# Cutting the last weight loads of a gated attention-and-MLP decode step, and turning its heads one block sooner

## The chip, the cores and the metric

The kernel runs on 1 core of one Trainium2 chip. The metric is the device time of one execution in microseconds (us), as the median of several; a profile of one execution stands beside it. A ratio of two kernels is the mean time of one kernel's fast runs over that of the other's in the same rounds, so it is not quite the ratio of the medians quoted. Engine names: PE is the matmul engine, PEld its weight loads, DVE, ACT and POOL the elementwise engines, SP the engine that issues the loads. "DMA engine" means one of the 16 that move the bytes.

## The reference, cut to what matters

```python
# x: 4 x 1 x 1024; k_cache, v_cache: 4 x 32 x 8192 x 128; wq: 1024 x 4096; wo: 4096 x 1024; bfloat16
g = sigmoid((x * gate_w).sum(-1))
q = x @ wq
o = softmax(q @ k_cache^T / sqrt(128)) @ v_cache       # per batch and head, one query
a = o.reshape(4, 1, 4096) @ wo                         # <- the change is in this product's loads
b = x + gated_mlp(x)                                   # 1024 -> 3584 -> 1024, scaled by a sigmoid
return g * a + (1 - g) * b                             # 4 x 1 x 1024
```

Two caches of 268 MB each are read once, so the step is a stream of loads with a little arithmetic on each byte. The product with wo is the last thing that happens.

## The kernel before: the parts that matter

wo is cut into 8 blocks (`NWB`) of 512 rows. A block is 4 rows (`FR`) of 1024 columns in each of 128 partitions, that is 8 KB a partition and 1 MB in all. Each of its rows takes two matmuls of 512 columns (`NH = 2`) that accumulate into `acc`.

```python
def wo_block(g, r0=0, r1=FR):
    ...                                                # a place w in the ring of buffers
    nc.sync.dma_start(out=w[:, r0:r1]..., in_=wov[:, g, r0:r1]...)
    def use():
        for r in range(r0, r1):
            for n in range(NH):
                mm_acc(n, LT[:, r, g, :], w[:, r, n * NB:(n + 1) * NB])
    return use
```

The left operand `LT` comes from the attention output: the V product lies in PSUM, ACT and DVE bring it to `OS`, `flush()` turns the V sums on PE (8 short matmuls, "led<-selg,OS"), `flush_late()` scales them into `OT`, and `o_rows()` turns the heads into `LT` (16 short matmuls, "led<-OT,identb"). The heads of the last V pairs are needed by blocks 6 and 7 alone (`GE = 6`). The end of the kernel:

```python
    last = [wo_block(g) for g in range(2, NWB - 2)]                       # blocks 2..5 whole
    cuts = [(NWB - 2, 0, 2), (NWB - 2, 2, 4), (NWB - 1, 0, 2), (NWB - 1, 2, 3), (NWB - 1, 3, 4)]
    last += [wo_block(*cut) for cut in cuts]                              # 6 in halves; 7: half, row, row
    flush_sums()
    for g in range(2, GE):
        last.pop(0)()
        if g == 3:
            flush(); flush_late()
        if g == 4:
            o_rows(GE, NWB)
    for use in last:
        use()
    res = [turned(Bn, NB) for _ in range(NH)]
    nc.vector.tensor_copy(out=res[0], in_=acc(0));  nc.sync.dma_start(out=out2[:, 0:NB], in_=res[0])
    nc.scalar.copy(out=res[1], in_=acc(1));         nc.scalar.dma_start(out=out2[:, NB:D], in_=res[1])
```

## Time and profile before

| | |
|---|---|
| time | 1343.43 us, median of 3 runs, 1343.15 to 1343.82 |
| span of the profiled execution | 1341.4 us |
| load queue, share of 16 DMA engines' span | 99.5% |
| busiest compute engine | PE, 79% |
| last wo row complete on every DMA engine | 1337.68 us |
| second half's copy out of PSUM (ACT) begins | 1338.37 us |

How to read it: the load queue is busy for 99.5% of the span and no compute engine for more than 79%, so I take the time as bytes over rate plus what happens after the last byte (576.13 MB, at a mean of 429 GB/s).

### The profile page before, as it was taken

The numbers are of one execution on the slowest core, as the hardware profiler recorded it, in microseconds if no ns is written. First come the engines' busy times: TensorE is split into PE (matmuls) and PEld (weight loads), VectorE is DVE, ScalarE is ACT, GpSimd is POOL, SyncE is SP. The second block draws the span as 40 slices with busy tenths as digits, with TensorE's granted clock in tenths as the row PEclk, the third lists the DMA queues.
The fourth block names the chain that finished last, engine by engine and source line by source line (L and its number), as shares of the span: only waits on it lengthen the run. The fifth ranks groups of instructions, "written<-read, shape, count | busy, mean of one in ns | idle before, by whom it ended". The sixth has DMA issues, their size and how long they took to land.

```text
span 1341.4 us, 6922 instructions
## 1 busy us (share of the span) xinstructions
PE 1057.9 (79%) x4608; PEld 138.4 (10%) x1396; DVE 638.3 (48%) x386; ACT 66.2 (5%) x99; POOL 71.8 (5%) x209
## 2 busy tenths in 40 slices
PE   2565877887778789787879778789697879888888
PEld 0000000001001010101001010101011011111111
DVE  2555988556544347454436256646145556100000
ACT  0000000200000000100000000100000000111000
POOL 2000000100000001000000000100000000100000
PEclk9777989898989898888899888889898889889989
DMA  9999999999999999999999999999999999999998
GB/s 415 434 434 436 435 436 424 445 425 428 436 436 427 440 434 423 442 428 434 438 427 434 432 436 434 434 430 423 436 431 439 436 421 441 430 427 430 427 427 335
DMA packets 14890, 576.13 MB, mean 429 GB/s; under 512 B 1662, under 2 KB 1670, under 8 KB 2316
## 3 DMA queue, kind: packets, MB, share of 16 engines
q1 hardware_dynamic: 14852, 575.69, 99.5%
q8 instruction: 23, 0.38, 0.1%
q14 instruction: 7, 0.06, 0.0%
q10 hardware_dynamic: 8, 0.00, 0.0%
HBM read 575.68 MB, written 0.01 MB: 429 GB/s over the span
## 4 chain that ended last, share of the span: by engine, by line
DMA 67%; DVE 21%; PE 11%; issue 0%; ACT 0%; SPq 0%; DVEq 0%
DMA ring<-in_A_k_cache_dram 51%; DVE TB L453 19%; DMA ring<-in_A_v_cache_dram 12%; PE o_ps L537 7%; PE S_ps L458 3%; DMA ring<-in_B_w_gate_dram 3%; DVE OS L558 2%; DMA ring<-in_A_wo_dram 1%; PE o_ps L320 0%; DVE PT L494 0%; DVE mx L480 0%; PE acc L286 0%; PE led L574 0%; PE o_ps L574 0%; DVE OS L566 0%
## 5 line engine op out<-in xcount | busy, mean ns | idle before, releaser
L453 DVE STREAM_TRANSPOSE TB<-ring 128x2048 uint32<-128x2048 uint32 x256 | 568.3, 2278 | 472.6 <-DMA ring<-in_A_k_cache_dram 464.5
L458 PE MATMUL S_ps<-TB,Z 128*128 128x512 bf16 x2048 | 532.6, 415 | 191.4 <-DVE TB L453 183.6
L537 PE MATMUL o_ps<-ring,PB 128*64 128x512 bf16 x2048 | 462.8, 388 | 50.3 <-DMA ring<-in_A_v_cache_dram 49.0
L458 PEld LDWEIGHTS <-Z 128*128 128x128 bf16 x512 | 53.1, 104 | 656.0 <-issue 656.0
L537 PEld LDWEIGHTS <-PB 128*64 128x64 bf16 x512 | 57.1, 112 | 449.1 <-issue 446.4
L513 POOL COPY PB<-PT 32x256 bf16<-32x256 bf16 x64 | 39.1, 611 | 712.5 <-PE o_ps L537 519.4
L566 DVE SCALAR_TENSOR_TENSOR OS<-o_ps,mE,OS 128x512 f32<-128x512 f32 x5 | 3.8, 750 | 138.9 <-ACT OS L564 138.9
L511 ACT COPY PB<-PT 32x256 bf16<-32x256 bf16 x64 | 39.6, 619 | 256.8 <-PE o_ps L537 251.0
L435 POOL COPY Z<-qa 32x4 bf16<-32x4 bf16 x128 | 25.8, 201 | 459.8 <-PE S_ps L458 432.2
L554 ACT ACTIVATE OS<-o_ps,mE 128x512 f32<-128x512 f32 x11 | 7.6, 687 | 450.9 <-PE o_ps L537 450.9
L558 DVE SCALAR_TENSOR_TENSOR OS<-o_ps,mE,OS 128x512 f32<-128x512 f32 x33 | 24.3, 737 | 1.5
L489 ACT ACTIVATE TB<-S_ps,mx 128x2048 bf16<-128x2048 f32 x4 | 7.9, 1967 | 331.6 <-DVE mx L486 331.6
L286 PE MATMUL acc<-ring,hT 128*4 128x512 bf16 x56 | 14.7, 432 | 5.4 <-ACT TB L489 5.4
L244 PE MATMUL S_ps<-identb,x 6*128 6x6 bf16 x8 | 0.6, 196 | 22.5 <-DMA x<-in_gate_w_dram 22.5
L286 PE MATMUL acc<-ring,LT 128*4 128x512 bf16 x64 | 14.8, 378 | 1.9 <-DMA ring<-in_A_wo_dram 1.2
L574 PEld LDWEIGHTS o_ps<-selg,OS 128*128 128x128 f32 x88 | 11.5, 191 | 9.3 <-issue 8.8
L494 DVE STREAM_TRANSPOSE PT<-TB 128x2048 bf16<-128x2048 bf16 x4 | 9.2, 2311 | 6.4 <-ACT TB L489 6.4
L480 DVE TENSOR_REDUCE mx<-S_ps 128x1 f32<-128x2048 f32 x4 | 9.1, 2282 | 6.2 <-PE S_ps L458 6.2
L320 PE MATMUL o_ps<-ring,xw 128*4 128x512 bf16 x112 | 9.0, 444 | 3.7 <-DMA ring<-in_B_w_gate_dram 3.7
L574 PE MATMUL o_ps<-selg,OS 128*128 128x8 f32 x88 | 10.5, 245 | 0.0
L586 DVE SCALAR_TENSOR_TENSOR OT<-led,sgb,rinv 128x8 bf16<-128x8 f32 x5 | 1.2, 236 | 19.1 <-PE led L574 19.0
L564 ACT ACTIVATE OS<-o_ps,mE 128x512 f32<-128x512 f32 x5 | 3.4, 687 | 128.9 <-PE o_ps L537 128.9
(73 smaller groups left out, 83.0 us busy)
## 6 DMA issues: line engine op xcount, KB each, us to landing
ring<-in_A_v_cache_dram SPq DMA_DIRECT2D x18, 4096.0 KB, 28.9
ring<-in_A_k_cache_dram SPq DMA_DIRECT2D x14, 4096.0 KB, 30.9
ring<-in_A_v_cache_dram SPq DMA_DIRECT2D x6, 2048.0 KB, 40.0
ring<-in_B_w_gate_dram SPq DMA_DIRECT2D x1, 7168.0 KB, 37.1
ring<-in_B_w_up_dram SPq DMA_DIRECT2D x1, 7168.0 KB, 37.1
ring<-in_B_w_down_dram SPq DMA_DIRECT2D x1, 7168.0 KB
ring<-in_A_wo_dram SPq DMA_DIRECT2D x6, 1024.0 KB, 19.8
ring<-in_A_v_cache_dram SPq DMA_DIRECT2D x4, 1024.0 KB, 28.3
```

Of the source, the lines that this page charges most:

```text
L286: nc.tensor.matmul(acc(n), lhsT=lhsT, rhs=rhs, start=start, stop=True, skip_group_check=True)
L320: nc.tensor.matmul(ps[32 * k:32 * k + Bn, z, :], lhsT=xT[TW * half + t], rhs=cols(w, t, 4 * z + k), start=(half + t == 0), stop=(half == 1 ...
L435: nc.gpsimd.tensor_copy(out=Z[at, :, QP - 1 + QP * q], in_=qa[at, :, h0 + q, b])
L453: nc.vector.transpose(out=flat_t.bitcast(U32).rearrange("p (j i) -> p j i", j=CJ), in_=kn[:, half].bitcast(U32))
L458: nc.tensor.matmul(sps[:, z, :], lhsT=Z[:, 2 * half + e, s:s + P], rhs=T[:, 16 * z:16 * z + 16, :, e], start=(t + n + half + e == 0), stop ...
L480: nc.vector.tensor_reduce(out=mx[:, 0:1], in_=sps[:].rearrange("p z n -> p (z n)"), axis=AX.X, op=ALU.max)
L494: nc.vector.transpose(out=PT[:].rearrange("p j i -> p (j i)"), in_=PTs)
L511: nc.scalar.copy(out=Bv[at, :, :, q, :], in_=Pv[at])
L513: nc.gpsimd.tensor_copy(out=Bv[at, :, :, q, :], in_=Pv[at])
L537: nc.tensor.matmul(o_ps[w // 2][row:row + NM, w % 2, :], lhsT=PB[:, RD * (d % NW) + n, z].rearrange("p w s j -> p (w s j)"), rhs=vn[:, j0 ...
L558: nc.vector.scalar_tensor_tensor(out=OS[:], in0=o_ps[w // 2][:, w % 2, :], scalar=mE[:, w:w + 1], in1=OS[:], op0=ALU.mult, op1=ALU.add)
L574: nc.tensor.matmul(oT, lhsT=OS[:, q * Dh:(q + 1) * Dh], rhs=selg[:, q].rearrange("p t s -> p (t s)"), start=(q == 0), stop=(q == 3), skip_ ...
```

## The change

Its intent: use the wo rows as they land, so that less PE work stands behind the last landing, and have the turning of V sums and heads out of the way earlier. Blocks 4 to 6 arrive in halves; block 7 as a half, a row, and the last row in two halves of its columns. The V sums are turned behind block 2 instead of 3, the heads behind block 3 instead of 4.

```diff
-    def wo_block(g, r0=0, r1=FR):
+    def wo_block(g, r0=0, r1=FR, half=None):
...
+            nc.sync.dma_start(out=w[:, r0, half * NB:(half + 1) * NB], in_=wov[:, g, r0, half * NB:(half + 1) * NB])
...
-                for n in range(NH):
+                for n in range(NH) if half is None else [half]:
...
-    last = [wo_block(g) for g in range(2, NWB - 2)]
-    cuts = [(NWB - 2, 0, 2), (NWB - 2, 2, 4), (NWB - 1, 0, 2), (NWB - 1, 2, 3), (NWB - 1, 3, 4)]
+    last = [wo_block(g) for g in range(2, 4)]
+    cuts = [(g, r, r + 2) for g in range(4, NWB) for r in (0, 2)][:-1] + [(NWB - 1, 2, 3)] + [(NWB - 1, 3, 4, n) for n in range(NH)]
...
-    for g in range(2, GE):
-        last.pop(0)()
-        if g == 3:
-            flush()
-            flush_late()
-        if g == 4:
-            o_rows(GE, NWB)
+    last.pop(0)()
+    flush()
+    flush_late()
+    last.pop(0)()
+    o_rows(GE, NWB)
```

More of the change, by code (lines that the diff above doesn't have):

```diff
@@ L392, in wo_block @@
         w = wo_home[home][:, at]
-        nc.sync.dma_start(out=w[:, r0:r1].rearrange("p r n -> p (r n)"),
-                          in_=wov[:, g, r0:r1].rearrange("p r n -> p (r n)"))
+        if half is None:
+            nc.sync.dma_start(out=w[:, r0:r1].rearrange("p r n -> p (r n)"),
+                              in_=wov[:, g, r0:r1].rearrange("p r n -> p (r n)"))
+        else:
+            nc.sync.dma_start(out=w[:, r0, half * NB:(half + 1) * NB], in_=wov[:, g, r0, half * NB:(half + 1) * NB])
         def use():
             for r in range(r0, r1):
-                for n in range(NH):
+                for n in range(NH) if half is None else [half]:
                     mm_acc(n, LT[:, r, g, :], w[:, r, n * NB:(n + 1) * NB])
```

## The prediction

> **What bounds the kernel now.** I read the page first: the busy times, the DMA queues, the chain.
>
> ```profile
> PE 1057.9 (79%) x4608; PEld 138.4 (10%) x1396; DVE 638.3 (48%) x386; ACT 66.2 (5%) x99; POOL 71.8 (5%) x209
> ...
> q1 hardware_dynamic: 14852, 575.69, 99.5%
> q8 instruction: 23, 0.38, 0.1%
> ...
> DMA 67%; DVE 21%; PE 11%; issue 0%; ACT 0%; SPq 0%; DVEq 0%
> ```
>
> The load queue kept the 16 DMA engines busy for 99.5% of the span. No compute engine is above 79%, so the DVE and PE shares of the chain are steps that a load waited for while other loads moved. 575.69 MB have to be read, and the change reads the same bytes. What is not transfer lies at the end of the span, so I followed the chain in order of time there.
>
> ```profile
> 1293.15 27.07 DMA ring<-in_A_v_cache_dram
> ...
> 1320.28 16.12 DMA ring<-in_A_wo_dram
> 1336.40 0.04 issue
> 1336.44 1.90 PE acc L286 x8
> 1338.35 0.02 issue
> 1338.37 0.57 ACT TB L637
> ```
>
> The span is 1341.4 us. Up to 1336.40 the chain is data arriving; then come 8 matmuls of the last wo block, one copy out of PSUM, and the output's DMA. Everything the change can win lies in these last 5 us, that is 0.4% of the time. The timeline of PE over the wo blocks:
>
> ```profile
> 1325.22 1.89 PE L286 MATMUL acc<-ring,LT 128*4 128x512 bf16 x8 [0.60 <-DMA ring<-in_A_wo_dram]
> 1327.72 1.89 PE L286 MATMUL acc<-ring,LT 128*4 128x512 bf16 x8 [0.61 <-DMA ring<-in_A_wo_dram]
> 1329.54 1.06 PE L574 MATMUL led<-selg,OS 128*128 128x8 f32 x8
> 1330.52 1.89 PE L286 MATMUL acc<-ring,LT 128*4 128x512 bf16 x8
> 1332.25 0.33 PE L381 MATMUL led<-OT,identb 128*32 128x8 bf16 x16
> 1332.69 5.64 PE L286 MATMUL acc<-ring,LT 128*4 128x512 bf16 x24
> ```
>
> Blocks 2 and 3 each wait about 0.6 us for their load. Then the turning of the V sums (1.06 us) and of the heads (0.33 us) makes PE a little late for blocks 4 and 5. The last row is blocks 5, 6 and 7 in one piece, and its length says whether PE ever caught up: a block of 8 takes 1.89 us, made of 7 starts 0.216 us apart and a last one of 0.38, so 24 without a wait would be 23 x 0.216 + 0.38 = 5.35 us. It took 5.64, so PE waited 0.29 us in it, and the chain puts that wait ahead of block 7, at 1336.40. **PE had caught up before the last block.** At last, the DMA in the same stretch (last two columns: share busy, GB/s):
>
> ```profile
> 1332.70:1334.50 1.80, 1.80 (x9) 0.34 (x4) 0.14 (x1) 0.00 (x0) 0.00 (x0) 1.00 0.62 250
> 1334.50:1336.40 1.90, 1.81 (x9) 0.34 (x4) 0.00 (x0) 0.00 (x0) 0.00 (x0) 1.00 0.49 196
> 1336.40:1338.40 2.00, 1.89 (x8) 0.25 (x3) 0.25 (x1) 0.03 (x1) 0.00 (x0) 1.00 0.10 39
> ```
>
> The engines do not finish together: from about 1332.7 on, some are done while the slowest still work. The trace's completion records[...] say it exactly: for every wo load the first and the sixteenth increment are 5.0 to 5.1 us apart, and the last wo row is complete on the slowest engine at 1337.68.
>
> [...] by the packet records a packet of 8192 B took 313 ns, 4096 B 159, 2048 B 84 and 1024 B 47 (medians), that is 26.2, 25.8, 24.4 and 21.8 GB/s for one engine, so size costs 2% at 4 KB[...]. [...] the page above shows 23 instruction packets of 0.38 MB on q8. Each took about 1.05 us on one DMA engine, and the spread between engines grows from 0.65 us at the first load to 5.1 at the end; that these fetches make the slowest engine is my inference.
>
> **The change part by part.**
> 1. *More, smaller loads.* The 11 wo loads become 14. Blocks 2 and 3 stay whole, 4 and 5 arrive in halves like block 6, block 7 in a half, a row, and two half rows. Each of the 16 engines has 8 partitions, so blocks 4 and 5 go from 16 packets of 8192 B to 32 of 4096 B, and the last row from 8 of 2048 B to 16 of 1024 B. From the packet medians: 32 x 159 - 16 x 313 = +80 ns, 16 x 47 - 8 x 84 = +80 ns, and three more completion writes of 9 ns. Packets overlap somewhat (8 of 2048 B would be 672 ns, the loads land 0.64 us apart; halves land 1.25 us apart and whole blocks 2.49), so by landings it is nearer 0.02 + 0.06. I take **+0.10 us** on the slowest engine; it is on the path, as that engine sets the end: last landing 1337.78.
> 2. *Fewer matmuls behind the last landing.* Before, the last row brings 2 matmuls: landing 1337.68, one at once, the next 0.216 later, with 0.38 until it is read, gives 1337.68 + 0.04 + 0.22 + 0.38 = 1338.32, and the copy started at 1338.37. The 8 from 1336.44 give 1336.44 + 1.89 = 1338.33: the two limits coincide by chance. After, one matmul follows the last half row: 1337.78 + 0.04 + 0.38 = 1338.20. **-0.15 us** against 1338.35, with part 1 already in it.
> 3. *V sums and heads turned one block sooner.* The 1.06 us now falls behind block 2, where OS is ready at 1327.09 (the last DVE step begins at 1326.40 and takes 0.69) and PE waits 0.6 us anyway; the 0.33 us falls behind block 3. PE's work is the same and PE is free sooner, but the 0.29 us that PE already waits ahead of block 7 swallows it: **0**. Its use is that blocks 4 to 6 are no longer late, so that the halves can be used as they land.
> 4. *Output.* The first half's copy (DVE, 0.68 us) may start a little sooner; the second (ACT, 0.57 us, then its DMA) is the later and moves with part 2. **0** more.
>
> Sum: -0.15 us of 1343.43, so 1343.28; I say **1343.3 us**. Where I chose: +0.10 for the packets instead of +0.19 from bare medians.
>
> **Rivals.**
> *Smaller loads starve the queue.* At most 8 loads are outstanding: each wo issue waits for the load eight earlier. With halves, eight loads hold fewer bytes. For it: the last issue now waits for the second half of block 4 (about 1330.2) rather than for block 2 (1325.18). Against: the slowest engine reaches those bytes only near 1337, 7 us later, and even the fastest, 5.1 us ahead, needs them at about 1332. If it did happen: +0.5 to +2 us.
> *PE is the true limit and the gain is larger.* For it: 24 matmuls in a row, PE busy throughout. Against: the 0.29 us wait, and after 1336.44 both limits agree to 0.02 us; PE can't end before the last landing. At most -0.3 us, if the smaller packets cost nothing.
> *Instruction fetches fall on other engines.* The instruction counts of PE are the same, so I expect the same pattern; if one more 1.05 us fetch fell on the slowest engine, or one fewer, the time moves by about 1 us either way, with no merit of the change. This is the largest source of error.
>
> **Range and chances.** The three runs before spread 1343.15 to 1343.82. The mechanisms are worth -0.3 to +0.1 us; the fetches and the spread of runs add some +-0.6 us. Range 1342.6 to 1344.1. Two per cent are 27 us; no mechanism here has more than 5 us to work on, so within 2% is 0.985, the rest is for a disturbed measurement.
>
> **What would show it.** Right: the chain is still DMA to about 1337.8 and ends in one matmul and the ACT copy; the timeline has the 1.06 us of turning at about 1327 and the 0.33 us before block 4; waits of PE for wo loads ahead of most halves, more of them than now; copy start near 1338.2. Wrong: a DMA share under 1 before 1332 with waits of the load queue for its own loads in its place (starved), a last landing later than 1338 (packet cost mis-sized), or a span changed by about 1 us with the spread of the completion increments changed as much (fetches).

The 0.216 us between matmuls is measured: in the trace of before the wo matmuls of a block start 215 to 216 ns apart, and one takes 376 to 379 ns. So are the packets: from the trace of before to that of the changed kernel, those of 8192 B go from 1280 to 1024, those of 4096 B from 384 to 896, those of 1024 B from 4 to 260, and those of 4 B (9 ns; I take them for the completion writes) from 1658 to 1706, 16 more for each of three more loads.

## The result, and the profile after

After: 1343.32 us, median of 6 runs (1343.03 to 1343.37). Before, in 6 runs of which 3 are new: 1343.24 us (1343.14 to 1343.82). The ratio of the fast runs is 0.9999, with a 95% interval of 0.9987 to 1.0012: the same. The span is 1341.3 us. The time came out as predicted, but the inside did not: the end of the computation came later, not sooner. The chain of the changed kernel, in order of time (start us, us, what):

```profile
1325.23 11.30 DMA ring<-in_A_wo_dram
1336.53 0.04 issue
1336.57 1.90 PE acc L286 x8
1338.47 0.02 issue
1338.49 0.58 ACT TB L638
```

It ends in the same way as before: eight matmuls, not one, behind a landing, and the copy 0.12 us later (1338.49 against 1338.37). PE's timeline says why eight:

```profile
1325.20 1.89 PE L286 MATMUL acc<-ring,LT 128*4 128x512 bf16 x8 [0.59 <-DMA ring<-in_A_wo_dram]
1327.13 1.06 PE L577 MATMUL led<-selg,OS 128*128 128x8 f32 x8
1328.12 1.89 PE L286 MATMUL acc<-ring,LT 128*4 128x512 bf16 x8
...
1330.18 3.66 PE L286 MATMUL acc<-ring,LT 128*4 128x512 bf16 x15
1334.06 1.02 PE L286 MATMUL acc<-ring,LT 128*4 128x512 bf16 x4 [0.22 <-DMA ring<-in_A_wo_dram]
1335.31 1.02 PE L286 MATMUL acc<-ring,LT 128*4 128x512 bf16 x4 [0.23 <-DMA ring<-in_A_wo_dram]
1336.57 1.89 PE L286 MATMUL acc<-ring,LT 128*4 128x512 bf16 x8 [0.23 <-DMA ring<-in_A_wo_dram]
```

The turning is where it was meant to be (1327.13), and PE now waits for the halves of block 6 as they land: 0.22 us of waiting, four matmuls, 0.23 us, four matmuls. But the last piece is eight without a gap. The first half of block 7 lands at 1336.53 and brings four matmuls; while PE does them the next row lands, then the half rows, each at or before the moment PE gets to it. So PE, not the last landing, sets the end, as it did before. The share of the DMA engines in the last stretches (last two columns) is that of before, a little higher at the end, which fits the move of the last landing from 1337.68 to 1337.83:

```profile
1332.70:1334.50 1.80, 1.48 (x8) 0.25 (x3) 0.00 (x0) 0.00 (x0) 0.00 (x0) 1.00 0.64 255
1334.50:1336.40 1.90, 1.61 (x7) 0.25 (x3) 0.00 (x0) 0.00 (x0) 0.00 (x0) 1.00 0.53 208
1336.40:1338.40 2.00, 1.83 (x8) 0.25 (x3) 0.13 (x1) 0.00 (x0) 0.00 (x0) 1.00 0.16 57
```

The copy is 0.12 us later while the span reads 0.1 us shorter: from the second output landing to the end of the span there were 1.10 us before and 0.90 us after. That part lies behind the program's own work and varies from look to look.

### The profile page after: what moved, and what is told of

Same layout as the page of the kernel before. It is cut to its first block, busy times and chain, and to the rows that moved or that the text cites. A ratio compares the mean times of both kernels' runs of the same rounds, so it can differ in the third digit from the quotient of the medians.

```text
span 1341.3 us, 6870 instructions
## 1 busy us (share of the span) xinstructions
PE 1052.3 (78%) x4550; PEld 138.5 (10%) x1396; DVE 638.3 (48%) x386; ACT 66.2 (5%) x99; POOL 71.5 (5%) x209
## 3 DMA queue, kind: packets, MB, share of 16 engines
q1 hardware_dynamic: 15284, 575.69, 99.6%
## 4 chain that ended last, share of the span: by engine, by line
DMA 67%; DVE 21%; PE 11%; issue 0%; ACT 0%; SPq 0%; DVEq 0%
DMA ring<-in_A_k_cache_dram 51%; DVE TB L456 19%; PE o_ps L540 8%; DMA ring<-in_A_v_cache_dram 7%; DMA ring<-in_A_wo_dram 6%; PE S_ps L461 3%; DMA ring<-in_B_w_gate_dram 3%; DVE OS L561 2%; PE o_ps L320 0%; DVE PT L497 0%; DVE mx L483 0%; PE acc L286 0%; PE led L577 0%; PE o_ps L577 0%; DVE OS L569 0%
## 5 line engine op out<-in xcount | busy, mean ns | idle before, releaser
L461 PE MATMUL S_ps<-TB,Z 128*128 128x512 bf16 x1990 | 526.3, 415 | 197.3 <-DVE TB L456 183.0
```

The costliest lines, as they stand in the source:

```text
L461: nc.tensor.matmul(sps[:, z, :], lhsT=Z[:, 2 * half + e, s:s + P], rhs=T[:, 16 * z:16 * z + 16, :, e], start=(t + n + half + e == 0), stop ...
```

## The experiments

Twelve runs were made: nine kernels, and second looks at three (before, changed, block 7 by rows). Differences of 0.1 us can't be seen in times that scatter by 0.3 us or more, so the verdicts of the small ones rest on events inside the traces. This table holds every look but the last experiment's, whose extra loads change the end; I come back to its columns below. "Half 7" is the landing of the first half of block 7 where there is one; landings are those of the slowest DMA engine, from the completion records of the traces (each of these loads makes 16 increments, and the core has 16 DMA engines; that each increment stands for one of them is my reading, as the records don't name them). PE takes a load up behind the sixteenth (before: 1336.40 and 1336.44); "spread" is first to sixteenth, at the last wo load. "Block 2" is the landing of all of block 2, "tail" the copy minus that landing, which takes out any shift that came earlier.

| kernel | spread | block 2 | half 7 | last landing | copy begins | copy - last landing | tail |
|---|---|---|---|---|---|---|---|
| before | 4.99 | 1325.18 | 1336.40 | 1337.68 | 1338.37 | 0.69 | 13.19 |
| before, second look | 5.91 | 1326.06 | 1337.23 | 1338.51 | 1339.20 | 0.69 | 13.14 |
| changed | 4.89 | 1325.16 | 1336.53 | 1337.83 | 1338.49 | 0.66 | 13.33 |
| changed, second look | 4.57 | 1325.12 | 1336.49 | 1337.81 | 1338.45 | 0.64 | 13.33 |
| order alone | 5.21 | 1325.22 | 1336.42 | 1337.71 | 1338.61 | 0.90 | 13.39 |
| loads alone | 5.75 | 1326.13 | 1337.40 | 1338.72 | 1339.37 | 0.65 | 13.24 |
| last row whole | 4.96 | 1325.15 | 1336.49 | 1337.76 | 1338.45 | 0.69 | 13.30 |
| block 7 by rows | 4.74 | 1324.94 | - | 1337.47 | 1338.19 | 0.72 | 13.25 |
| block 7 by rows, second look | 4.56 | 1324.88 | - | 1337.43 | 1338.11 | 0.68 | 13.23 |
| block 7 by rows, PE kept busy | 5.10 | 1325.48 | - | 1338.03 | 1338.48 | 0.45 | 13.00 |
| all whole | 5.11 | 1325.08 | - | 1337.42 | 1339.39 | 1.97 | 14.31 |
| all by rows | 1.04 | 1325.17 | - | 1338.49 | 1339.16 | 0.67 | 13.99 |
| more PE instructions | 6.46 | 1326.50 | 1337.68 | 1338.96 | 1339.64 | 0.68 | 13.14 |

The theory (A): the copy begins at the later of two moments, the first half of block 7 plus eight matmuls, or the last landing plus the matmuls that it brings. The change moved only the second. The rival (C), which is the form that my prediction used: the last landing decides.

### The order alone

Loads as before, the turning sooner:

```diff
-        if g == 3:
+        if g == 2:
             flush()
             flush_late()
-        if g == 4:
+        if g == 3:
             o_rows(GE, NWB)
```

> The loads of the kernel before, with V sums and heads turned one block sooner. Theory A (the end is set by the landing of the first half of block 7 plus its 8 matmuls): last matmuls start at about 1336.44 and the ACT copy at 1338.37, as before, because PE waited 0.29 us there anyway; PE now waits ahead of blocks too, 0.5 us or more in all. Rival B (being sooner frees PE for the end): copy 0.2 us or more sooner.

1343.64 us, copy at 1338.61, and PE waits for no load at all in the tail. PE had come late out of the V phase (its block 2 began at 1326.09, 0.87 us behind its landing at 1325.22), and then stood still once more:

```profile
1326.09 1.89 PE L286 MATMUL acc<-ring,LT 128*4 128x512 bf16 x8
1328.67 1.06 PE L574 MATMUL led<-selg,OS 128*128 128x8 f32 x8 [0.70 <-DVE OS L568]
...
1331.72 6.85 PE L286 MATMUL acc<-ring,LT 128*4 128x512 bf16 x31
```

The late V phase made `OS` late as well (its last DVE step ended at 1328.61), and the sooner turning waits for `OS` right behind block 2; from block 3 on everything ran back to back. The expected wait for loads was not there, so this look doesn't tell the theories apart; it shows a third state, PE as the limit by lateness, which the experiments with block 7 by rows take up. Here the order even cost time: without the 0.70 us, PE would have been back at the limit of block 7's first half, 1336.42 + 1.96 = 1338.38, so the copy 0.23 us sooner. That is an estimate from this trace; no run has the old order with PE as late and the loads on time.

### The loads alone

```diff
     last.pop(0)()
+    last.pop(0)()
     flush()
     flush_late()
     last.pop(0)()
+    last.pop(0)()
     o_rows(GE, NWB)
```

> The smaller loads of the change with V sums and heads turned at the places of before. Theory A: each block cut in two costs the slowest DMA engine about 0.07 us, so block 7's first half lands near 1336.53 and the copy starts near 1338.49, as in the changed kernel; PE a little late for blocks 4 and 5, caught up by block 7. Rival B (the order carries a gain that the loads give back): copy 0.2 us or more later than in the changed kernel, so 1338.7.

1344.31 us, copy at 1339.37. The absolute numbers are about 0.9 us late because the loads were: block 2 itself landed at 1326.13, long before any of the loads that differ are used. Relative to that, all is as in the changed kernel: the last matmuls start 0.04 us behind the half's landing after a wait of 0.20 us, the copy comes 1.97 us behind that landing (1.96 in the changed kernel), and the tail is 13.24 against 13.33 us. Turning later made PE late for block 4, and PE had still caught up before block 7:

```profile
1337.45 1.89 PE L286 MATMUL acc<-ring,LT 128*4 128x512 bf16 x8 [0.20 <-DMA ring<-in_A_wo_dram]
```

**When PE is not late out of the V phase, the order is worth nothing: a wait ahead of block 7 swallows it.** Rival B falls.

### The last row whole

```diff
- ... + [(NWB - 1, 2, 3)] + [(NWB - 1, 3, 4, n) for n in range(NH)]
+ ... + [(NWB - 1, 2, 3), (NWB - 1, 3, 4)]
```

> The changed kernel with its last row in one load instead of two column halves. Theory A (8 matmuls behind the first half of block 7 are the limit): copy start unchanged at 1338.49, within 0.05. Rival C (the last landing is the limit, which my prediction assumed): one matmul more behind it, so the copy 0.15 to 0.2 us later, 1338.65.

1343.37 us, copy at 1338.45, which is the changed kernel's 1338.49 and 1338.45 in its two looks. PE's last piece:

```profile
1336.53 1.89 PE L286 MATMUL acc<-ring,LT 128*4 128x512 bf16 x8 [0.23 <-DMA ring<-in_A_wo_dram]
```

**The column halves of the last row bought nothing.** Against rival C this look says less than it was meant to. Its 1338.65 took the last landing as unmoved, but without the halves it came at 1337.76, and two matmuls behind that end at 1337.76 + 0.04 + 0.22 + 0.38 = 1338.40; the eight that PE begins at 1336.53 end at 1336.53 + 1.89 = 1338.42. The two limits coincide again, as in the kernel before. What speaks against C is the changed kernel itself: one matmul behind its last landing would end at 1337.83 + 0.04 + 0.38 = 1338.25 (1338.23 in the second look), and the copy began at 1338.49 (1338.45), behind eight matmuls without a gap.

### Block 7 by rows

Blocks 2 to 5 whole, 6 in halves, 7 in rows, the last one in column halves:

```diff
-    last = [wo_block(g) for g in range(2, 4)]
-    cuts = [(g, r, r + 2) for g in range(4, NWB) for r in (0, 2)][:-1] + [(NWB - 1, 2, 3)] + [(NWB - 1, 3, 4, n) for n in range(NH)]
+    last = [wo_block(g) for g in range(2, NWB - 2)]
+    cuts = [(NWB - 2, 0, 2), (NWB - 2, 2, 4)] + [(NWB - 1, r, r + 1) for r in range(3)] + [(NWB - 1, 3, 4, n) for n in range(NH)]
```

> Blocks 2 to 5 whole, 6 in halves, 7 row by row with its last row in column halves, turned sooner. Theory A: no block is cut where that only costs packets, and only 2 to 4 matmuls wait behind any landing of block 7; last landing near 1337.76, one matmul, copy at 1338.2, that is 0.15 to 0.2 us before the kernel before and 0.3 before the changed one. The time then 1343.1, within the noise of either. Rival C: the same as the changed kernel, 1338.5.

1343.13 us, median of 5 runs (1342.73 to 1343.42), against 1343.32 of before in the same rounds; ratio 0.9999, interval 0.9985 to 1.0012. The copy begins at 1338.19, as theory A has it, but not for its reason: PE was late again and ran its last 31 matmuls without a wait, and the loads themselves were 0.24 us early.

> Block 7 row by row once more; in the first look PE came late out of the V phase and ran all 31 matmuls without a wait, so the loads were not what limited it. Theory A: if PE is on time now, it waits ahead of rows, and the copy starts 0.40 to 0.45 us after the last landing, or at most 0.65 us; if it is late again, 0.7 us after.

> The changed kernel once more, to see what differs between executions of one kernel. Theory A: whatever the absolute times, the copy starts 1.92 us after PE takes up the first half of block 7, unless PE came late out of the V phase at half clock (as in the look at the kernel with the order alone changed), in which case the matmuls run without a wait and the copy may be up to 0.2 us later. Spread 5 or 6.2 us, the span 1.0 to 1.2 us longer in the second case.

Block 7 by rows: 1343.04 us, copy at 1338.11, PE late once more. The changed kernel: 1343.15 us, copy at 1338.45, 1.92 us behind the start of the last matmuls at 1336.53, exactly as in its first look. The lateness has a cause that the clock column shows (the column before the last two), here in the second look at block 7 by rows, in two stretches right after PE had idled from about 1284 to 1288:

```profile
1290.00:1292.00 2.00, 2.00 (x6) 0.42 (x3) 0.00 (x0) 0.00 (x0) 0.00 (x0) 0.50 0.98 418
1294.00:1296.00 2.00, 2.00 (x7) 0.18 (x1) 0.00 (x0) 0.00 (x0) 0.00 (x0) 0.50 0.98 414
```

PE ran at half its clock until about 1297. In the kernel before, the clock also fell to 0.50 in that wait (eight V matmuls at 1288.33 took 3.48 us, against 1.89 for the eight at 1322.74, at 1.00), but was back by 1292. All the looks fall in line with it: in the five where full clock was back by 1292 (both at before, both at changed, all whole) PE waited 0.59 or 0.60 us for block 2, that is, it was on time; in the eight where it came back at 1296 to 1298 PE waited 0.35 us at most or was late. The order of the turning adds to it: in both looks at block 7 by rows PE, late by 0.7 us at block 2, then waited another 0.70 us for `OS`, as in the order alone. By these traces PE would otherwise have been done before the last landing. Block 7 by rows with the old order was not run.

### Block 7 by rows, with PE kept busy

Added to the same kernel, ahead of the V pair before the last:

```diff
+        if (kind, d) == ("v", ND - 2):
+            for _ in range(16):
+                nc.tensor.matmul(A_ps[1][:, 1, :], lhsT=identb[:], rhs=Zt[0][:].rearrange("p a b -> p (a b)")[:, 0:NB],
+                                 start=True, stop=True, skip_group_check=True)
```

> Block 7 row by row, and 16 matmuls without use written to a PSUM bank that is free, ahead of the V pair before the last, where PE idles 4 to 5.6 us and its clock then falls to half. Theory A (PE came late out of that stretch and was the limit in both looks at block 7 row by row): PE clock 0.9 or more from 1290 on, PE waits for loads in the tail again, copy 0.42 to 0.65 us after the last landing, near 1337.9, 0.2 us sooner than without. Rival: the clock falls anyway and nothing changes, or the added matmuls run at half clock and push PE 3 us later, copy at 1338.2 or later. Time 1342.9 to 1343.2, within noise.

1343.18 us, median of 5 runs (1342.82 to 1343.30), against 1343.31 of before in the same rounds; ratio 0.9998, interval 0.9984 to 1.0011. The same two stretches, and PE's last blocks:

```profile
1290.00:1292.00 2.00, 2.00 (x14) 1.07 (x9) 0.24 (x1) 0.00 (x0) 0.00 (x0) 1.00 1.02 434
1294.00:1296.00 2.00, 2.00 (x11) 0.22 (x2) 0.00 (x0) 0.00 (x0) 0.00 (x0) 1.00 1.08 455
```

```profile
1330.49 1.89 PE L286 MATMUL acc<-ring,LT 128*4 128x512 bf16 x8
1332.98 5.46 PE L286 MATMUL acc<-ring,LT 128*4 128x512 bf16 x24 [0.60 <-DMA ring<-in_A_wo_dram]
```

The clock stays at 1.00, PE is on time and waits for block 5 again, and the copy begins 0.45 us behind the last landing, the shortest in the table and what one matmul behind a landing should give (0.04 + 0.38 and the step to the copy). It is a near thing: the 24 matmuls took 5.46 us, and without any wait would have taken 5.35. The tail is 13.00 us, 0.17 less than the mean of before. Here the form "last landing plus one matmul" holds. The absolute copy was 1338.48 all the same, because in this execution the loads landed 0.54 to 0.60 us later than in the two looks without the added matmuls. The added matmuls brought PE on time and so took away the wait for `OS` too; how much each of the two is worth is not separated. The whole gain is within what the loads move by themselves.

### All whole, and all by rows

Two amplified versions: six loads of 1 MB, or 24 of 256 KB.

```diff
# all whole
+    last = [wo_block(g) for g in range(2, NWB)]
+    cuts = []
# all by rows
+    cuts = [(g, r, r + 1) for g in range(2, NWB) for r in range(FR)]
+    last = [wo_block(*cut) for cut in cuts]
```

> All six last wo blocks whole. Theory A: last landing sooner, near 1337.5, but 8 matmuls behind it: 1337.5 + 0.04 + 1.89 = 1339.4, copy 1.0 to 1.1 us later than before, time about 1344.4. If the size of the last load did not matter for the end (rival D, the span is set by transfer alone): copy within 0.2 us of before and time 1343.2.

> All six last wo blocks row by row (24 loads of 256 KB), so the cost of small packets is amplified and at most 2 MB are outstanding. Theory A (packet cost on the slowest engine by the packet medians, 184 ns a whole block): last landing 0.9 to 1.0 us later than before, near 1338.6, copy near 1339.2, time near 1344.2; fast engines run dry, so the spread of the 16 completion increments falls under 5 us with no cost of its own. Rival E (starved queue): last landing 2 us or more later, DMA share well under 1 from 1325 on, time over 1345. Rival F (small packets hidden): last landing within 0.3 us of before.

All whole: 1344.28 us, median of 4 runs, against 1343.14 before in the same call. The last landing is the earliest in the table, and the copy 1.02 us later than before, because a whole block stands behind it:

```profile
1335.01 1.89 PE L286 MATMUL acc<-ring,LT 128*4 128x512 bf16 x8 [0.55 <-DMA ring<-in_A_wo_dram]
1337.47 1.89 PE L286 MATMUL acc<-ring,LT 128*4 128x512 bf16 x8 [0.57 <-DMA ring<-in_A_wo_dram]
```

So cutting the last block does pay, about 1 us, and the kernel before had already collected it. Rival D falls.

All by rows: 1344.23 us, median of 4 runs. The last landing is 1338.49, 0.81 us later than before; the packet medians had said 0.95. The chain, from the last wo landings on:

```profile
1332.59 5.30 DMA ring<-in_A_wo_dram
1337.89 0.04 issue
1337.93 0.59 PE acc L286 x2
1338.52 0.01 issue
1338.53 0.61 PE acc L286 x2
```

Two matmuls behind each landing, no backlog. And the spread of the 16 increments fell from 5 to 1.04 us: with eight loads of 256 KB outstanding the fast DMA engines ran dry (DMA share 0.86 from 1320 to 1325, against 1.01 in the kernel before), which cost nothing, as the slowest one was never without work (its loads kept landing 0.68 us apart, 8 packets of 84 ns). Rivals E and F fall: small packets cost about what their durations say.

By the times alone neither version is told from before with certainty (ratios 1.0007, interval 0.9992 to 1.0022, and 1.0008, 0.9991 to 1.0024), since two of the seven runs of before in that call were near 1344.2 themselves. The next experiment is about those.

### More PE instructions

In the kernel before, two of the four K matmuls of each group are cut into two of 256 columns:

```diff
+                    first = t + n + half + e == 0
+                    for z, lo, hi in ((0, 0, 16), (1, 0, 16), (2, 0, 16), (3, 0, 16)) if first else \
+                            ((0, 0, 8), (0, 8, 16), (1, 0, 8), (1, 8, 16), (2, 0, 16), (3, 0, 16)):
+                        nc.tensor.matmul(sps[:, z, 32 * lo:32 * hi], lhsT=..., rhs=T[:, 16 * z + lo:16 * z + hi, :, e], ...)
```

> The kernel before with half of the K matmuls cut into two of 256 columns: about 1020 more PE instructions, 4 more instruction fetches (27), the same data. In the traces each fetch throws one DMA engine 1.1 to 1.5 us behind, and the seven that are last at the end look hit three times. Theory G (fetches make the slowest engine): three engines are hit a fourth time, spread at the end 6.2 to 6.7 us, everything from the last V loads on 1.1 to 1.5 us later, time 1344.3 to 1344.9. Rival H (spread is of the engines themselves): spread 5.1 us, time 1343.2 to 1343.5.

1344.66 us, median of 4 runs (1344.57 to 1344.86), against 1343.14; ratio 1.0009, interval 0.9994 to 1.0024, so the times alone don't decide, though all four lie above all seven of before (at most 1344.24). From the page, its PE busy time and its instruction queue:

```profile
PE 1064.1 (79%) x5624; PEld 139.5 (10%) x1396; DVE 638.2 (48%) x386; ACT 66.2 (5%) x99; POOL 71.4 (5%) x209
...
q8 instruction: 27, 0.44, 0.1%
```

PE is busy 6 us longer in 1342, spread over the whole; the tail is 13.14 us, as before. But the spread is 6.46 us and block 2 lands 1.32 us later than in the first look at before. Step by step it can be followed in the kernel before too: a load complete at 503 us had a spread of 1.99 us, a fetch ran at 519, and a load complete at 543 had 3.08; one at 989 had 3.53, a fetch ran at 992, and one at 1009 had 4.65. Increment by increment, each of these two fetches moved one of the sixteen later by 1.5 us (from 1.55 to 3.08 us behind the first, and from 3.11 to 4.65). The packet records agree: each of the two fetches took 1.07 us, and the 64 KB packet of the load queue that began as it ended took 2.92 us in place of the median of 2.42; over all 23 fetches the two parts come to 1.44 to 1.57 us. **In the kernel before, an instruction fetch held one DMA engine back by about 1.5 us, and PE had to wait for the engine furthest behind (block 7's half: increments from 1331.34 to 1336.40, PE from 1336.44).** Rival H falls. That the furthest behind is the one hit most often is likely, but the increments don't name their engines. The second look at the kernel before belongs here:

> The kernel before once more, for the spread of its own tail from execution to execution: Theory A has its last matmuls 1.90 us behind the start of block 7 and the copy at 1338.3 to 1338.6 (0.12 before the changed kernel's where both are on time), or 1.1 us later if the spread of increments is 6.2 us.

1344.28 us, with 23 fetches but a spread of 5.91 us, and everything from block 2 on 0.8 to 0.9 us late, while its tail is 13.14 us. So the same program loses or keeps that 1 us from one execution to the next. It also means that the 1.32 us of the four added fetches is not their pure cost: against this second look block 2 came 0.44 us later. The look at the loads alone had the same bad luck (spread 5.75, 0.95 us late at block 2). What moves the extra hold-up onto the slowest engine in some executions is open.

### Which DMA engines are late

Six loads of 1, 2, 4, 8, 12 and 14 partitions behind the last wo load of the changed kernel:

```diff
+    for k in (1, 2, 4, 8, 12, 14):
+        scr = const.tile([k, 64], BF, name=f"scr{k}")
+        nc.sync.dma_start(out=scr[:], in_=A_wo[0:k, 0:64])
```

> The changed kernel with six loads of 1, 2, 4, 8, 12 and 14 partitions by 128 bytes behind its last wo load. [...] Theory G (instruction fetches fall on 8 engines in turn): the increments of the load on 8 engines are either all among the seven or eight late ones, or all among the early ones, or (every second engine) half and half. The time 0.1 to 0.3 us longer, as small loads stand at the end of the queue.

1344.06 us, 0.8 us over one run of before instead of 0.1 to 0.3: PE was late again, with the 0.70 us wait for `OS`, and block 2 landed at 1325.64. As a map it was mostly a miss: at most eight loads are outstanding (in the changed kernel the last four wo loads are issued 0.06 to 0.07 us behind the landing of the load eight earlier), so the probes were issued late, after most engines had drained. What can be said: the load of 4 partitions was complete at 1335.82; of the load of 8, six increments came by 1337.00 and two at 1337.40 and 1337.80; the last wo load was complete at 1338.30. Which engines a small load runs on is not shown here, so the increments can't be laid on particular engines, and that fetches fall on 8 engines in turn stays my guess, not shown either. The full map is open, and with it whether bytes could be moved off the late engines.

## Why the prediction was right, and where its working was wrong

**The bound: right.** The load queue stayed at 99.6%, and nothing in this change reached more than 0.2 us.

**Part 1, more and smaller loads: the mechanism right, its size too small.** I chose +0.10 us over the +0.19 that the bare packet medians gave, because packets overlap (8 of 2048 B are 672 ns, the loads land 0.64 us apart). From block 2's landing to the last landing the kernel before took 12.50 and 12.45 us, the changed one 12.67 and 12.69: +0.20 us. The loads alone, with the very same loads, had 12.59, so +0.12 to +0.22 by look and +0.18 in the mean of the three (last row whole: 12.61). The bare medians were nearer than my choice; all by rows, 0.81 us for the 0.95 of the medians, does not speak against it. By landings, loads of 1 MB came 2.49 us apart, 421 GB/s, those of 512 KB 1.25 us, 419 GB/s, and those of 256 KB in all by rows 0.68 us, 386 GB/s.

**Part 2, fewer matmuls behind the last landing, -0.15 us: the step that failed.** I worked out that two limits coincided before the change (1338.32 and 1338.33), then computed the end after the change from the one that the change relaxes, and forgot the other. The eight matmuls behind the first half of block 7 were untouched: 1336.53 + 0.04 + 1.92 = 1338.49, which is the measured copy. The last landing with its one matmul would have allowed 1338.25. In the kernel all whole, eight matmuls behind a landing cost 1 us in the open, and block 7 by rows with PE on time shows the other limit, at 0.45 us behind the last landing. Two of the prediction's own signs of being right, one matmul at the end of the chain and a copy near 1338.2, did not come. (The 0.216 us a matmul held: a stream of 31 without a wait took 6.85 us, and 30 x 0.216 + 0.38 = 6.86.)

**Part 3, the order: right, 0, when PE is on time,** and for the reason given, the wait ahead of block 7. The loads alone show it. What the part missed: when PE came late out of the V phase, `OS` was late too, and the sooner turning made PE wait 0.70 us for it (order alone, block 7 by rows twice, all by rows, and the last experiment). A small misreading beside it: PE was not late for block 5 in the kernel before; that block landed at 1332.65 and PE took it up at 1332.69.

**Part 4, the output: right that it adds nothing.** The ACT copy stayed the later one; the first half's copy did not start sooner but 0.12 us later (1338.27 against 1338.15).

**The sum.** In place of -0.15 us the traces have +0.12 at the copy in the first pair and +0.17 in the tail (13.33 and 13.33 against 13.19 and 13.14). Against the scatter of the runs both are nothing, so a wrong sign left the time right: 1343.32 for 1343.3. That the number was met is luck as far as the mechanism goes; any forecast of no visible change would have met it.

**The rivals.** The starved queue did not happen; even 24 loads of 256 KB did not starve the engine that counts. PE as the true limit I had put at "both agree"; it was the rival to take seriously. That instruction fetches make the slowest engine was an inference then; that they push engines back is now shown, fetch by fetch, and the kernel with four more was 0.4 to 1.3 us later at block 2 than the two looks at before.

**Where the expected gain went.** Of the 1 us that cutting the last block can give, the kernel before had nearly all. The rest, 0.17 us in the tail of one look, came with block 7 in rows and PE on time together; that version ran, and its time (1343.18 against 1343.31) is the same within noise.

## What to carry to other kernels

When two limits end at the same moment, a change that moves one of them gains nothing: write the end as the later of both, and recompute both after the change. Cut a load only as finely as the work behind it asks for, and first where the backlog starts (here the first half of the last block), not at the very last piece. Moving work ahead of a wait is safe only if its input is ready in the late executions too (here `OS`). And before polishing 0.1 us at the end, look at how far apart the DMA engines finish; here it was 0.65 us at the first load and 5 us at the last (1.04 to 6.46 over the kernels), and it moved by 1 us between executions of one program.
